# In a visit to the array's quarters, k^T v's even chunks go off the diagonal and its odd ones on it

## The chip, the cores and the metric

The kernel runs on one core of a Trainium2 chip. A core has five engines that run side by side: TensorE (PE in the profile; its weight loads are listed apart as PEld), VectorE (DVE), ScalarE (ACT), GpSimd (POOL) and SyncE (SP, which here mostly issues DMA transfers). TensorE multiplies a stationary operand, loaded beforehand, with a moving one and adds the products up in PSUM, a memory of eight banks. SBUF is the larger memory that all engines work from. The metric is the device time of one execution in microseconds (us), lower is better.

## The reference

Two blocks follow each other. The first is a linear attention without softmax, followed by an RMS norm; the second is a feed-forward block with a gate:

```python
kv  = np.einsum('bhsd,bhse->bhde', k, v)          # q, k, v: (8, 8, 576, 64)
out = np.einsum('bhsd,bhde->bhse', q, kv)
rms = np.sqrt(np.mean(out * out, axis=-1, keepdims=True) + 1e-06)
x   = (out / rms * g_norm)                        # then (B,H,S,D) -> (B*S, H*D) = (4608, 512)
h = x @ w_in                                      # (512, 2048)
sp = np.maximum(h, 0.0) + np.log1p(np.exp(-np.abs(h)))
y = (h * erf(sp)) @ w_out                         # (2048, 512)
```

All is fp32. For each batch element and head, `kv` is a 64 x 64 matrix, summed over 576 rows of k and v.

## The kernel before, in words

**Rows.** Tokens are worked in nine groups of 512 (`NG = B + 1`): for each of the eight batch elements its first 512 rows, and a ninth group made of the last 64 rows of all eight. The groups are numbered T, and `attention(T, p)` does the attention of a pair of heads p (four pairs) of group T. While the feed-forward block works on group T, the attention of group T + 1 is prepared in pieces set between its steps, one pair of heads per quarter of the group.

**Feed-forward.** Groups 0 and (in part) 1 run as plain fp32 products (lines 1021 and 655). From then on operands are split into two fp32r parts and a third form, and each product is twelve matmuls of 128 x 512 (line 599, `product`): eight into a bank called `n_ps`, four into one called `m_ps`. Six PSUM banks are used in turn. ScalarE and VectorE clear them (lines 1192, 574, 569), apply the gate and cut the results for the second product. The weights in their three forms are kept in DRAM and loaded again for each group, on SP's DMA queue (`load_parts`, line 844).

**The visit.** Everything that the change touches lies in `visit()` inside `attention`, which TensorE reaches once for each pair of heads of groups 1 to 7, 28 times in all. Its output `at` is a PSUM tile of two banks. All its matmuls contract over 64 partitions (one head of the pair) and give 64 output partitions, so each uses one quarter of the 128 x 128 array: the quarter is named by the head whose rows go in (`rows_of[i]`) and by the half of the output partitions. Two quarters are on the diagonal (rows of head i to output half i), two off it (head i to half 1 - i). TensorE is given, in this order:

1. four products `kv^T q^T` of 64 x 256 (line 411), "the quarters": first two off the diagonal into bank 0, then two on it into bank 1;
2. two products of 64 x 64 for the last 64 rows of the batch element, "the tail" (line 419), both on the diagonal, into bank 1;
3. eighteen products of 64 x 64 (lines 425 and 343, `kv_products`), which make k^T v for the *next* pair of heads: nine chunks c of 64 rows, each for both heads i. A chunk lies either on the diagonal (and goes to bank 1) or off it (bank 0). The 28th visit has no next pair and leaves these out.

All products on one side add up in PSUM to a partial sum. VectorE later adds the partial sums of the two sides (`kv_kept`: two copies at line 360 and an addition at line 361), whichever chunks each holds. `kv_products` is also called by `prepare` (line 370), once, ahead of the first visit, and by `first_group` (line 702) for the four pairs of group 0; these calls have no quarters and no tail ahead of them.

**What sets the order.** The order is that of the program (a manual schedule): each engine gets its instructions in the order in which Python issues them, and waits on semaphores of the others. After the visit come ScalarE's square (line 430), VectorE's halving of the square (lines 447 and 448), the copy of the tail (line 433), `kv_kept`, and, a step later, the mean over 64 features on TensorE (lines 463 and 464) and the norm. TensorE itself goes on after the visit with the next product of the feed-forward block, which uses the whole array.

Of the kernel before, what the change touches and what calls it, by code (L numbers as in the profile page):

```python
# [68 lines left out]
def kernel(  # L69
# [253 lines left out]
    def halves_of(t):  # L323
        return t.rearrange("p (a t) -> p a t", a=2)
# [10 lines left out]
            qT = ready[T, p] = qt_tile("qT")  # L335
            nc.vector.transpose(out=qT, in_=q_sb.pop((T, p)))

    def kv_products(T, p, at):


        ks, vs = (x.pop((T, p)) for x in (k_sb, v_sb))
        for c in range(CH):
            for i, rows in enumerate(rows_of):
                half = (i + c) % 2
                yield partial(
                    nc.tensor.matmul,
                    at[rows_of[half], 1 if half == i else 0, kv_cols],
                    lhsT=ks[rows, c],
                    rhs=vs[rows, c],
                    start=(c < 2),  # L350
                    stop=(c >= CH - 2),
                )
# [10 lines left out]
    def at_tile():  # L363
        return at_pool(1).tile([P, 2, G], FP32, name="at_ps", tag="at")

    def prepare(T, p):

        at = at_tile()
        for product_ in kv_products(T, p, at):
            product_()  # L370
        kept.append(partial(kv_kept, T, p, at))
# [7 lines left out]
    def attention(T, p, in_parts=False):  # L379
# [6 lines left out]
        then = divmod(T * NP + p + 1, NP)  # L386

        def two(t):
            return halves_of(t) if quad else t
# [14 lines left out]
        def visit():  # L404


            qT = ready.pop((T, p))
            at = st["at"] = at_tile()
            x = halves_of(qT[:, 0:G])
            for a, i in ((0, 0), (0, 1), (1, 0), (1, 1)):  # L410
                nc.tensor.matmul(  # L411
                    at[rows_of[i if a else 1 - i], a, 0 : 2 * P],
                    lhsT=bd[rows_of[i], a * D : (a + 1) * D],
                    rhs=x[rows_of[i], a],
                    start=True,
                    stop=True,
                )
            for s in rows_of:
                nc.tensor.matmul(
                    at[s, 1, 2 * P : 2 * P + R], lhsT=bd[s, D : 2 * D], rhs=qT[s, G:S], start=True, stop=True  # L420
                )
            st["o"] = at[:, :, 0 : 2 * P]
            if then[0] < B:
                for product_ in kv_products(*then, at):
                    product_()  # L425
            if apart:
                st["sq"] = x_new.tile([P, G], FP32, name="sq", tag="x")
            else:
                st["sq"] = qT[:, 0:G]
            nc.scalar.activation(two(st["sq"]), st["o"], AF.Square)  # L430
# [94 lines left out]
        if apart:  # L525
            pieces = ((loads,), (visit, halve, keep_tail), (then_,))
            return (*(partial(chain, *group) for group in pieces), mean, norm, *after)
        pieces = (first_, (visit, loads), (halve, keep_tail) if halves else (keep_tail,))
        return (*(partial(chain, *group) for group in pieces), mean, partial(chain, norm, then_), *after)

# [163 lines left out]
    def first_group(p):  # L694
# [4 lines left out]
        def kv():  # L699
            st["kv"] = at_tile() if p == 0 else ps_now[0].tile([P, 2, G], FP32, name="kv_ps", tag="at")  # L700
            for product_ in kv_products(0, p, st["kv"]):
                product_()
# [273 lines left out]
    for n in range(FIRST * FC + 1):  # L976
        T, f = divmod(n, FC)
# [165 lines left out]
    for m in range(first_batch, batches + 1):  # L1143
        T, b = divmod(m, NB)
# [141 lines left out]
```

## Time and profile before

| what | value |
|---|---|
| time, median of 3 runs | 902.89 us (902.69 to 903.44) |
| span of the profiled execution, first to last instruction | 901.3 us |
| mean granted TensorE clock | 0.999 |
| TensorE busy, share of the span | 893.6 us, 99% |
| VectorE busy | 766.7 us, 85% |
| ScalarE busy | 595.1 us, 66% |
| mean of one record of line 425 (k^T v in a visit) | 221 ns |
| distance between visits, groups 3 to 7 | 23.81 us |

The profiled execution is one run, and of its time the page gives the span; the timed runs also hold what lies around it. In the rows that follow, a group of instructions stands with its line, engine, operation, the names of output and inputs, the shape, how often, and after the bar the busy time in us, the mean of one in ns, and the idle time of its engine just before it. An fp32 matmul stands in the trace as two records, each with its own weight load: 18 products of a visit are 36 records, and 27 visits make 972. Matmuls overlap, so the duration of a record isn't its cost: what counts is the distance from one start to the next.

### The profile page before, as it was taken

The page shows a single profiled execution, that of the slowest core. Times are in us where ns is not written, and L with a number is a line of the kernel's source. Part 1 is how long each engine was busy: PE and PEld are TensorE (multiplying, and loading weights), DVE is VectorE, ACT ScalarE, POOL GpSimd, SP SyncE. Part 2 cuts the span into 40 slices and gives each one's busy share as a digit, 9 for nine tenths or more (in the row PEclk, how much of TensorE's full clock was granted, in tenths as well). Part 3 has the DMA queues.
Part 4 walks back from the last instruction along what each step waited for, and adds up shares of the span by engine and source line. Part 5 has one row for each costly group of instructions (what it writes and reads, how often), then busy time and mean ns, then how long its engine had stood idle before and what let it go on. Part 6 is the DMA issues. An engine that isn't in the chain of part 4 may idle for free.

```text
span 901.3 us, 13468 instructions
## 1 busy us (share of the span) xinstructions
PE 893.6 (99%) x4962; PEld 672.4 (75%) x4962; DVE 766.7 (85%) x1105; ACT 595.1 (66%) x789; POOL 4.7 (1%) x14
## 2 busy tenths in 40 slices
PE   8999999999999999999999999999999999999998
PEld 4444456666788888888888888888888888888887
DVE  5899978899799888888888888888888888886667
ACT  5976687777766666666766666666666666665552
POOL 2000000000000000000000000000000000000000
PEclk9999999999999999999999999999999999999999
DMA  9977418899699987988899979988897787778871
GB/s 285 295 224 226 108 73 319 305 341 355 233 384 355 347 301 258 382 308 297 273 361 336 320 248 335 365 300 292 286 341 273 270 304 309 286 282 323 317 263 51
DMA packets 136929, 259.89 MB, mean 288 GB/s; under 512 B 78816, under 2 KB 87264, under 8 KB 136864
## 3 DMA queue, kind: packets, MB, share of 16 engines
q1 hardware_dynamic: 136128, 258.09, 81.3%
q8 instruction: 39, 0.64, 0.3%
q10 hardware_dynamic: 544, 0.82, 0.3%
q14 instruction: 26, 0.21, 0.1%
q0 software_dynamic: 192, 0.13, 0.0%
HBM read 224.40 MB, written 34.60 MB: 287 GB/s over the span
## 4 chain that ended last, share of the span: by engine, by line
PE 96%; DMA 1%; DVE 1%; ACT 1%; issue 0%; SPq 0%; DVEq 0%
PE n_ps L599 50%; PE m_ps L599 25%; PE o_ps L655 9%; PE h_ps L1021 5%; PE at_ps L425 2%; PE at_ps L411 2%; PE n_ps L918 1%; PE at_ps L463 1%; PE at_ps L464 1%; DMA q_sb<-in_q_dram 1%; DMA w_raw<-in_moe_w_out_dram 1%; PE o_ps L918 0%; DVE w_e L276 0%; PE o_ps L722 0%; DVE w_in_sb L281 0%; PE ms_ps L729 0%
## 5 line engine op out<-in xcount | busy, mean ns | idle before, releaser
L599 PE MATMUL n_ps<-w_out_parts,g_forms 128*128 128x512 f32 (+1 forms) x936 | 230.7, 389 | 0.0
L599 PE MATMUL n_ps<-x_forms,w_in_parts 128*128 128x512 f32 x896 | 223.9, 392 | 0.0
L599 PEld LDWEIGHTS n_ps<-w_out_parts,g_forms 128*128 128x128 f32 x936 | 173.7, 188 | 35.3
L599 PEld LDWEIGHTS n_ps<-x_forms,w_in_parts 128*128 128x128 f32 x896 | 166.6, 188 | 35.3
L574 DVE TENSOR_TENSOR h<-m_ps,h 128x512 f32<-128x512 f32 x116 | 78.2, 687 | 60.3 <-PE m_ps L599 58.1
L599 PE MATMUL m_ps<-w_out_parts,g_forms 128*128 128x512 f32 x464 | 124.0, 389 | 0.0
L599 PE MATMUL m_ps<-x_forms,w_in_parts 128*128 128x512 f32 x448 | 119.7, 389 | 0.0
L1192 ACT ACTIVATE h<-n_ps 128x512 f32<-128x512 f32 x112 | 66.2, 594 | 75.1 <-PE n_ps L599 75.0
L1197 ACT ACTIVATE s<-h 128x512 f32<-128x512 f32 x112 | 68.3, 629 | 70.0 <-DVE h L574 70.0
L599 PEld LDWEIGHTS m_ps<-w_out_parts,g_forms 128*128 128x128 f32 x464 | 87.1, 188 | 18.5
L599 PEld LDWEIGHTS m_ps<-x_forms,w_in_parts 128*128 128x128 f32 x448 | 84.1, 188 | 17.5
L574 DVE TENSOR_TENSOR e<-m_ps,e 128x512 f32<-128x512 f32 x116 | 80.2, 692 | 15.2 <-PE m_ps L599 5.3
L655 PE MATMUL o_ps<-w_out_sb,h_sb 128*128 128x512 f32 x192 | 86.8, 595 | 0.0
L540 DVE SCALAR_TENSOR_TENSOR g_forms<-g_forms 128x1024 fp32r<-128x1024 f32 x58 | 71.1, 1225 | 2.0
L537 DVE TENSOR_TENSOR g_forms<-h,g_forms 128x1024 fp32r<-128x1024 f32 x58 | 70.6, 1217 | 1.2 <-ACT g_forms L534 1.1
L534 ACT ACTIVATE g_forms<-h 128x1024 fp32r<-128x1024 f32 x58 | 58.4, 1049 | 15.5 <-PE m_ps L599 11.1
L569 DVE SCALAR_TENSOR_TENSOR e<-n_ps,e 128x512 f32<-128x512 f32 (+1 forms) x89 | 60.4, 678 | 6.9 <-PE n_ps L599 6.9
L1246 DVE TENSOR_TENSOR h<-h,s 128x1024 f32<-128x1024 f32 x56 | 65.9, 1218 | 0.0
L655 PEld LDWEIGHTS o_ps<-w_out_sb,h_sb 128*128 128x128 f32 x192 | 35.5, 190 | 38.3 <-issue 36.9
L1021 PE MATMUL h_ps<-xT,w_in_sb 128*128 128x512 f32 x128 | 57.9, 596 | 1.1 <-DVE w_in_sb L281 1.1
L115 ACT ACT_TABLE_LOAD x43 | 55.2, 1283 | 0.8
L1220 ACT ACTIVATE s<-s 128x1024 f32<-128x1024 f32 x50 | 50.6, 1053 | 0.3
(148 smaller groups left out, 1018.7 us busy)
## 6 DMA issues: line engine op xcount, KB each, us to landing
w_out_parts<-w_out SPq DMA_DIRECT2D x116, 768.0 KB, 6.8
w_in_parts<-w_in SPq DMA_DIRECT2D x112, 768.0 KB, 6.7
w_in<-w_new SPq DMA_DIRECT2D x16, 768.0 KB, 4.9
k_sb<-in_k_dram SPq DMA_DIRECT2D x32, 288.0 KB, 5.9
v_sb<-in_v_dram SPq DMA_DIRECT2D x31, 288.0 KB, 5.8
w_raw<-in_moe_w_in_dram SPq DMA_DIRECT2D x16, 512.0 KB, 5.9
w_raw<-in_moe_w_out_dram SPq DMA_DIRECT2D x8, 1024.0 KB, 5.1
out_dram<-e SPq DMA_DIRECT2D x32, 256.0 KB, 3.8
```

The lines of the kernel that those rows point to most:

```text
L115: nc.scalar.preload_act_table_set("softplus")
L534: nc.scalar.activation(high, x, AF.Copy, scale=1.0 + 2.0**-13)
L537: nc.vector.tensor_tensor(out=low, in0=x, in1=high.bitcast(FP32), op=ALU.subtract)
L540: nc.vector.scalar_tensor_tensor(out=both, in0=low.bitcast(FP32), scalar=SHIFT, in1=high.bitcast(FP32), op0=ALU.mult, op1=ALU.add,)
L569: nc.vector.scalar_tensor_tensor(out=out_, in0=ps, scalar=scale, in1=out_, op0=ALU.mult, op1=ALU.add)
L574: nc.vector.tensor_tensor(out=out_, in0=ps, in1=out_, op=ALU.add)
L599: nc.tensor.matmul(ps[:, cols], lhsT=weights(form, k), rhs=moving(form, k)[:, cols], start=(form == forms[0] and k == 0), stop=(form == fo ...
L655: nc.tensor.matmul(o_ps[j], lhsT=g[:, j * P : j * P + P], rhs=one(w_out_sb, f), start=(f == 0), stop=last,)
L1021: nc.tensor.matmul(plain[i], lhsT=blocks_of(one(w_in_sb, i % FC))[:, c], rhs=xT[T][:, c, :], start=(c == 0), stop=(c == KC - 1),)
L1192: nc.scalar.activation(h[:, i], n_ps, AF.Copy, scale=SHIFT - 1.0)
L1197: nc.scalar.activation(s[:, i], h[:, i], AF.Softplus)
L1246: nc.vector.tensor_tensor(out=part(h, half), in0=part(h, half), in1=part(s, half), op=ALU.mult)
```

## The change

The call of `kv_products` in the visit gets `first=1`, which turns the sides around: chunks 0, 2, 4, 6 and 8 go off the diagonal, into bank 0, and chunks 1, 3, 5 and 7 on it, into bank 1. The tail stays on the diagonal. The other callers keep `first=0`. The number of instructions of every kind, their shapes, their operands in SBUF and their order in the program stay as they were.

```diff
-    def kv_products(T, p, at):
+    def kv_products(T, p, at, first=0):
 
         ks, vs = (x.pop((T, p)) for x in (k_sb, v_sb))
         for c in range(CH):
             for i, rows in enumerate(rows_of):
-                half = (i + c) % 2
+                half = (i + c + first) % 2
                 yield partial(
                     nc.tensor.matmul,
                     at[rows_of[half], 1 if half == i else 0, kv_cols],
                     lhsT=ks[rows, c],
                     rhs=vs[rows, c],
                     start=(c < 2),
                     stop=(c >= CH - 2),
                 )
...
             if then[0] < B:
-                for product_ in kv_products(*then, at):
+                for product_ in kv_products(*then, at, first=1):
                     product_()
```

## The prediction

> **What bounds the kernel now.** I read the page's busy times first, then the chain of work that ended last, then the groups of the visit's three lines, and last the timeline around single visits. From the page:
>
> ```profile
> span 901.3 us, 13468 instructions
> PE 893.6 (99%) x4962; PEld 672.4 (75%) x4962; DVE 766.7 (85%) x1105; ACT 595.1 (66%) x789; POOL 4.7 (1%) x14
> PE 96%; DMA 1%; DVE 1%; ACT 1%; issue 0%; SPq 0%; DVEq 0%
> ```
>
> TensorE is busy for 99% of the span and makes 96% of the chain, so time taken from TensorE comes off the end, as long as nothing else becomes late. The groups by shape (busy us, mean ns, idle before):
>
> ```profile
> L425 PE MATMUL at_ps<-v_sb,k_sb 64*64 64x64 f32 x972 | 23.0, 221 | 0.0
> L411 PE MATMUL at_ps<-qT,bd_kv 64*64 64x256 f32 x224 | 18.6, 402 | 0.0
> L419 PE MATMUL at_ps<-qT,bd_kv 64*64 64x64 f32 x112 | 7.9, 217 | 0.0
> ```
>
> Line 425 costs 23.0 us over 27 visits, 0.85 us each; this is where the change can take from. TensorE's timeline of one visit of the steady part (start us, length us, records):
>
> ```profile
> 287.76 0.66 PE L411 MATMUL at_ps<-qT,bd_kv 64*64 64x256 f32 x8
> 288.26 0.22 PE L419 MATMUL at_ps<-qT,bd_kv 64*64 64x64 f32 x2
> 288.27 0.27 PE L425 MATMUL at_ps<-v_sb,k_sb 64*64 64x64 f32 x2
> 288.32 0.23 PE L419 MATMUL at_ps<-qT,bd_kv 64*64 64x64 f32 x2
> 288.37 0.75 PE L425 MATMUL at_ps<-v_sb,k_sb 64*64 64x64 f32 x34
> 289.05 0.50 PE L599 MATMUL n_ps<-x_forms,w_in_parts 128*128 128x512 f32 x1
> ```
>
> Two records of line 425 start between the tail's first and second pass. The tail and chunk 0 share the diagonal quarters, so these two can only be chunk 1, off the diagonal: it overtook chunk 0. The record with chunk 0's semaphore wait, a weight load at 554 ns (counted, as all ns below, from the visit's first product at 287.764), says the same. So each quarter of the array works off its own products, and the visit lasts as long as the longer of two chains. Its end, in the same view with the window moved, so that the first number is the start of the earliest record still running:
>
> ```profile
> 288.73 0.40 PE L425 MATMUL at_ps<-v_sb,k_sb 64*64 64x64 f32 x9
> 288.78 0.34 PE L425 MATMUL at_ps<-v_sb,k_sb 64*64 64x64 f32 x6
> 288.90 0.23 PE L425 MATMUL at_ps<-v_sb,k_sb 64*64 64x64 f32 x2
> ```
>
> The last six records fill three places, two records each, where earlier places hold four: at the end only the diagonal works. And the visit without k^T v:
>
> ```profile
> 692.97 0.28 PE L419 MATMUL at_ps<-qT,bd_kv 64*64 64x64 f32 x4
> 693.18 0.50 PE L599 MATMUL n_ps<-x_forms,w_in_parts 128*128 128x512 f32 x1
> ```
>
> There the whole-array product comes 148 ns after the last small start (559 to 707 ns in the rows); with k^T v it is also 148 (1142 to 1290). So the end of the visit is the last small start plus a fixed emptying of the array.
>
> **The change part by part.** *The two chains now.* On the diagonal, starts (first of two heads) are 496 and 552 (tail, two passes), then 610, 669, 727, 785, 844, 902, 960, 1019, 1077, 1135 (five chunks, two passes each): twelve places, 58.3 ns apart once running. Off the diagonal: 509, 615, 674, 732, 790, 849, 907, 965 (four chunks): eight places, done three places early. The change removes one chunk, two places, from the diagonal and adds two places off it: ten and ten. Nothing else is added or removed; no DMA, no instruction of VectorE, ScalarE or SP changes or moves in its queue.
>
> *Diagonal after.* It loses its last two places and ends with 1019 (second head 1025): 1142 - 1025 = 117 ns earlier.
>
> *Off the diagonal after.* The unknown is when chunk 0 starts. Its quarters begin the second pass of the big products at 267 and 274; the diagonal's begin at 280 and 287, and the tail follows 216 ns later (496 - 280 = 503 - 287), its weights having been loaded beside them at 282 and 289. By the same step chunk 0 starts at 267 + 216 = 483, its second pass 56 later (as 496 to 552), and eight more places give 483 + 56 + 8 x 58.3 = 1005; second head 1012. The diagonal, at 1025, then sets the end: saving 117 ns, the upper bound. Lower bound: the weights come as late as chunk 1's do now (507 ns, right behind the tail's second load at 504). Then the places are 509, 615 and eight more: 615 + 8 x 58.3 = 1081, second head 1088, saving 54 ns.
>
> I take 117. What held chunk 1 back to 507 was how far TensorE reaches over unissued records. At 507 it passed 10 (the two tail matmuls, eight records of chunk 0); at 854 chunk 7's first load passed 11; before 496 it would have had to pass 14 and did not. In the new order chunk 0 stands directly behind the tail: at 282 it has at most 8 ahead (one big matmul, seven of the tail). That is inside what the rows show as passable. k and v are there: their loads land microseconds before, and chunk 1 of the same tiles is read at 509 now.
>
> The Trainium skill, "TensorE: Matmul & The Clock Gate", Part 3 (packing small matmuls), says that matmuls start and end strictly in program order, and that a weight load overlaps running matmuls only in other row groups. Both speak against this forecast: chunk 0 would wait for the tail's second pass at 559, start about 561 and end near 1090, worth some 52 ns a visit or 1.35 us in all, 901.5 us. The trace disagrees on both: chunk 1 starts at 509, ahead of the tail's 552; and the tail's loads at 282 run beside big products on the same rows (267, 280).
>
> *What waits for the visit.* ScalarE's square, VectorE's copies and the release of k's and v's buffers wait for the visit's last product and can come 117 ns earlier; nothing queues behind a new wait. For the rest, cover must last: VectorE is busy 398.5 of the 452.3 us from 240.2 to 692.5, ScalarE 295.5, and TensorE 452.3, with no idle gap. The weight loads land at least 2.6 us ahead of first use there, and they are triggered mostly by TensorE's own progress. If that cover were gone, at most the saving itself would be lost.
>
> *One visit gives nothing.* After the first visit (at 41.5 us) TensorE waits for VectorE; the chain there:
>
> ```profile
> 49.87 1.24 DVE w_in_sb L281
> 51.15 1.12 PE h_ps L1021 x2
> ```
>
> TensorE sat idle 0.39 us for it, and that VectorE chain comes from a DMA issued by SP at 42.34, not from the visit; the first 117 ns only lengthen the wait. From 51.15 on the chain is TensorE's to the last stretch.
>
> *Sum.* 26 visits x 0.117 = 3.04 us; 26 x 0.054 = 1.40 us at the lower bound; 27 x 0.117 = 3.16 at the upper. The profiled span of 901.3 would become 898.3. The median of the timed runs, 902.89, stands 1.6 us above that span, for what lies around it, which the change leaves alone: 902.89 - 3.04 = 899.85.
>
> **The rivals.** *A, the forecast:* 899.85 us.
>
> *B, late start off the diagonal:* chunk 0's first weight load carries the wait on a DMA's semaphore, and no row shows such a load taken ahead of older ones. If it isn't, it goes at 507, in order. Against it: at 139.27 a load of line 599 with a wait is issued 1 ns after the matmul before it starts. 902.89 - 1.40 = 901.49 us, 0.16% faster.
>
> *C, the change does not show in the time:* something other than the chains holds the next product, which has a semaphore wait of its own at 1289. For it: VectorE and ScalarE, which it waits for, are busy through the visit. Against it: it comes 148 ns after the last small start in every visit, with and without k^T v; a foreign wait would scatter. 902.9 us.
>
> *D, slower:* four quarters working at once run at a longer place than two, and the change makes ten such places of eight. At the start of the program the four places of group 0 (5.15 to 5.63) are 107 ns apart. At that distance ten places (nine distances, 963 ns) take the place of the present twelve (1135 - 496 = 639 ns): 324 ns more, 26 x 0.324 = 8.4 us, 911.3 us. It decides from about 79 ns a place, (639 + 69) / 9, where 69 ns a visit is 0.2%. Against it: in that same group the distance falls to 58 by 5.71 with four records a place; the same eighteen products ahead of the first visit (37.12) run at 58, four at once, and so do the eight shared places in this visit.
>
> **How the numbers follow.** About 0.2%, 1.8 us, is what a measurement of this kernel can tell from no change. A has 0.74, B 0.15, C 0.07, D 0.04. A is faster; B and C are within the bound; D is slower; a little of B lies between the two bounds of the start and beyond 0.2%: faster 0.75, same 0.21, slower 0.04. A's own range is 899.4 to 900.5 (27 visits and the runs' spread below, a chain start some 20 to 40 ns late above). To leave out no more than 2 in 10 I take in B: 899.4 to 901.7.
>
> **What would show it.** In the profile after, line 425 begins ahead of line 419 in the timeline, about 483 ns after the first quarter; the last places hold four records; the next product comes at 1173 ns instead of 1290; visits in the steady part are 23.69 us apart instead of 23.81. Line 425's busy time stays near 23 us or less, since it begins sooner but ends earlier. A start at 509 and a next product near 1236 would show B; places longer than 58 ns, D; a gap above 148 ns, C. The forecast is wrong if TensorE takes a waiting load only in order, or if VectorE's chain in groups 1 and 2, where it is busy 82.9 of 93.4 us, sets the pace instead.

## The result

The changed kernel is faster by 0.23%: 900.96 us (median of 12 runs, 900.4 to 901.16) against 902.93 us (12 runs), ratio 0.9977, 95% interval 0.9969 to 0.9986. Two later sessions gave 0.9975 (0.9966 to 0.9984) and 0.9973 (0.9962 to 0.9985). The saving is 2.0 to 2.5 us; 3.04 had been forecast. The result lies inside the range that was given (899.4 to 901.7), 1.1 us above the forecast of 899.85.

### The profile after

From the page; the span was 901.3 before:

```profile
span 899.1 us, 13468 instructions
PE 891.6 (99%) x4962; PEld 670.6 (75%) x4962; DVE 765.5 (85%) x1105; ACT 594.8 (66%) x789; POOL 4.7 (1%) x14
PE 97%; ACT 2%; DVE 1%; issue 0%; DVEq 0%; ACTq 0%
```

TensorE is 2.0 us less busy and still makes the chain. The groups by shape:

```profile
L425 PE MATMUL at_ps<-v_sb,k_sb 64*64 64x64 f32 x972 | 20.5, 218 | 0.0
L411 PE MATMUL at_ps<-qT,bd_kv 64*64 64x256 f32 x224 | 18.6, 402 | 0.0
L419 PE MATMUL at_ps<-qT,bd_kv 64*64 64x64 f32 x112 | 7.9, 217 | 0.0
```

Only line 425 moved: 23.0 to 20.5 us, its mean from 221 to 218 ns. The timeline of the same visit on TensorE (first product at 287.131):

```profile
287.13 0.66 PE L411 MATMUL at_ps<-qT,bd_kv 64*64 64x256 f32 x8
287.61 0.22 PE L425 MATMUL at_ps<-v_sb,k_sb 64*64 64x64 f32 x2
287.63 0.22 PE L419 MATMUL at_ps<-qT,bd_kv 64*64 64x64 f32 x2
287.67 0.23 PE L425 MATMUL at_ps<-v_sb,k_sb 64*64 64x64 f32 x2
287.68 0.23 PE L419 MATMUL at_ps<-qT,bd_kv 64*64 64x64 f32 x2
287.73 0.65 PE L425 MATMUL at_ps<-v_sb,k_sb 64*64 64x64 f32 x32
```

Chunk 0 now starts ahead of the tail, and a first and second pass of each alternate. Row by row, in ns from the visit's first product, the weights of chunk 0 are loaded at 268 and 275, its products start at 482 and 489, the tail's at 496 and 502, the last four of the visit at 1005, 1011, 1018 and 1025, and the next whole-array product at 1173. The forecast had 483, 1005, 1025 and 1173. All 27 visits show the same, within 1 or 2 ns.

So where is the rest of the 3.04 us? The busy times by stage, cut at the first visit, at the ninth (where the steady part begins) and at the last. The columns are the stretch and its length, then the busy time (and number of instructions) of PE, PEld, VectorE, ScalarE and GpSimd, and at the end the granted clock, the busy share of the DMA engines and the GB/s that they moved. Before:

```profile
41.48:240.15 198.67, 198.05 (x961) 114.30 (x961) 176.65 (x268) 147.59 (x210) 0.00 (x0) 1.00 0.69 235
240.15:692.48 452.33, 452.33 (x2814) 370.19 (x2813) 398.52 (x571) 295.52 (x381) 0.00 (x0) 1.00 0.91 319
692.48:901.30 208.82, 205.19 (x921) 170.01 (x920) 164.38 (x210) 122.27 (x154) 0.00 (x0) 1.00 0.72 270
```

After:

```profile
41.64:239.70 198.06, 197.32 (x961) 113.58 (x960) 176.48 (x268) 147.46 (x210) 0.00 (x0) 1.00 0.68 235
239.70:690.26 450.56, 450.56 (x2814) 368.50 (x2813) 397.61 (x571) 295.40 (x382) 0.00 (x0) 1.00 0.92 321
690.26:899.10 208.84, 205.19 (x921) 170.00 (x920) 164.29 (x210) 122.25 (x154) 0.00 (x0) 1.00 0.71 270
```

The steady part lost 1.77 us over 19 distances between visits, 93 ns each and not 117, and TensorE has no idle gap in it either way. From visit to visit the distances changed so: first to second +4 ns; the next three -133, -118 and -117; the three after these, in group 1's feed-forward, only -40 each; then -120; then nineteen at -93. Set row beside row, the matmuls that follow are longer. In the steady part, before and after, the first feed-forward product behind the visit, and the start of the one behind it:

```profile
289.05 2.11 PE L599 MATMUL n_ps<-x_forms,w_in_parts 128*128 128x512 f32 x8
291.91 0.84 PE L599 MATMUL n_ps<-x_forms,w_in_parts 128*128 128x512 f32 x3
```

```profile
288.30 2.12 PE L599 MATMUL n_ps<-x_forms,w_in_parts 128*128 128x512 f32 x8
291.18 0.84 PE L599 MATMUL n_ps<-x_forms,w_in_parts 128*128 128x512 f32 x3
```

The twelve matmuls take 2.852 us before and 2.875 after (by the rows' ns). Their distances settle at 226.7 ns. Before, the first is 338 and those that follow 236, 228, 232, 231, then 227; after, the first is 335, then 235, 233, 236, 224, 231, 236, 228, 233, 231, and only then 227. Added up over the ten behind the first, that is 20 to 21 ns above the settled pace before and 46 to 47 after, 23 ns net of the 2 to 3 saved on the first. In the three distances of -40 the same happens on a larger scale: the first split product behind the visit (a few plain ones of line 655 come ahead of it) runs at 225 and 228 ns in turn before, at 234 and 239 after; 77 of the 117 ns go there. Together 3 x 77 + 19 x 23 = 0.67 us are given back; this loss is called the give-back below, and the 20 to 21 or 46 to 47 ns above the settled pace the excess.

### The profile page after: what moved, and what is told of

It reads as the page before. It is cut to its first block, busy times and chain, and to the rows that moved or that the text cites. A ratio compares the mean times of both kernels' runs of the same rounds, so it can differ in the third digit from the quotient of the medians.

```text
span 899.1 us, 13468 instructions
## 1 busy us (share of the span) xinstructions
PE 891.6 (99%) x4962; PEld 670.6 (75%) x4962; DVE 765.5 (85%) x1105; ACT 594.8 (66%) x789; POOL 4.7 (1%) x14
## 4 chain that ended last, share of the span: by engine, by line
PE 97%; ACT 2%; DVE 1%; issue 0%; DVEq 0%; ACTq 0%
PE n_ps L599 50%; PE m_ps L599 25%; PE o_ps L655 9%; PE h_ps L1021 5%; PE at_ps L411 2%; PE at_ps L425 2%; PE n_ps L918 1%; PE at_ps L463 1%; PE at_ps L464 1%; PE warm_ps L802 1%; PE o_ps L918 0%; ACT w_m L260 0%; PE o_ps L722 0%; DVE w_in_sb L281 0%; DVE w_e L276 0%
```

## The experiments

The question left was what decides the give-back: how the visit ends (two quarters at work or four), how short it is, or when it ends. The kernels ran in three sessions, each on another chip and each with the kernel before beside them. Of the first four kernels there is one timed run each, so that their times say little and the argument rests on their traces; of the others there are 6 to 11.

**The tail left out, sides as before.**

```diff
-            for s in rows_of:
-                nc.tensor.matmul(
-                    at[s, 1, 2 * P : 2 * P + R], lhsT=bd[s, D : 2 * D], rhs=qT[s, G:S], start=True, stop=True
-                )
...
-                out=x_last[:, p, T * R : T * R + R], in_=st["at"][:, 1, 2 * P : 2 * P + R]
+                out=x_last[:, p, T * R : T * R + R], in_=st["at"][:, 1, 0:R]
```

The copy behind the visit then reads columns that the quarters wrote, in the tail's place.

> The kernel before with its sides as they were, but the tail's two products of the visit are left out (the last 64 rows of each batch element then come out of other numbers). Chain theory: the diagonal falls from twelve places to ten, 496 to 1018/1025 ns after the visit's first product, off the diagonal stays at eight; the next product at 1173 ns, as in the changed kernel, though no chunk has changed sides. Rival (the changed kernel is faster because four quarters, not two, are at work at the end): the visit loses less than 117 ns. On the give-back behind the visit (9 to 11 products some ns longer, 23 ns in the steady part): if it hangs on when the visit ends, the first distance is 335 ns and the excess of the next ones over 226.7 is 46 ns, as in the changed kernel; if it hangs on the diagonal working alone at the end, 337 to 338 and 20 to 21 ns, as in the kernel before.

```profile
287.73 0.66 PE L411 MATMUL at_ps<-qT,bd_kv 64*64 64x256 f32 x8
288.21 0.76 PE L421 MATMUL at_ps<-v_sb,k_sb 64*64 64x64 f32 x36
288.90 0.50 PE L595 MATMUL n_ps<-x_forms,w_in_parts 128*128 128x512 f32 x1
```

Measured: last start 1025, next product 1173 ns in every visit; 335 ns and 46 to 47 behind it; 23713 ns from visit to visit in the steady part, the changed kernel's figure to the nanosecond. The diagonal worked alone for the last places here, as in the kernel before, and still the give-back was the changed kernel's. So the saving is the length of the longer chain, whichever products are taken off it, and the give-back does not come from the quarters that are at work at the end. The time, 901.46 us against 903.2, holds 0.67 us lost in one wait, told of below.

**Odd chunks ahead of even ones.** In the changed kernel:

```diff
-        for c in range(CH):
+        order = (1, 0, 3, 2, 5, 4, 7, 6, 8) if first else range(CH)
+        for n, c in enumerate(order):
```

> The changed kernel, ten places on each side, with chunk 1 (on the diagonal) issued ahead of chunk 0 (off it), 3 ahead of 2 and so on. If what lets chunk 0 start at 483 is that it stands within TensorE's reach behind the tail, it now stands behind 16 records and starts at 509 without weights loaded ahead: last start near 1088, next product near 1236 ns, 63 ns a visit and 1.7 us in all lost against the changed kernel. If balance alone counts and the order does not, 1173 ns and the changed kernel's time.

```profile
287.24 0.66 PE L412 MATMUL at_ps<-qT,bd_kv 64*64 64x256 f32 x8
287.73 0.22 PE L420 MATMUL at_ps<-qT,bd_kv 64*64 64x64 f32 x2
287.75 0.27 PE L426 MATMUL at_ps<-v_sb,k_sb 64*64 64x64 f32 x2
...
288.48 0.50 PE L600 MATMUL n_ps<-x_forms,w_in_parts 128*128 128x512 f32 x1
```

The first two records of k^T v start behind the tail's and last 0.27 us, as in the kernel before; the next product came at 1236 to 1237 ns. With the same ten places on each side, the order alone costs 63 ns in the visit. Here the semaphore's wait stands with chunk 1 on the diagonal, and chunk 0, free of any wait, is late all the same: it is the distance in the queue that holds it back. The kernel without the tail says the same from the other side: there chunk 1 off the diagonal had 11 unissued records ahead of it, chunk 0's with the wait among them, its weights were loaded at 268 all the same, and its first product started at 483. That the wait does no harm is shown by the changed kernel, where the load at 268 carries it. The give-back was gone, though: 337 to 338 ns and 20 to 21 behind the visit, so the distance between visits is 23753 ns, only 40 above the changed kernel's. Time 901.67 us against 903.2.

**One more product per quarter.** Ahead of k^T v in the changed kernel's visit (for two more, the range is 2):

```diff
+                spare = slice(2 * P + R + D, 2 * P + R + 2 * D)
+                ks, vs = k_sb[then], v_sb[then]
+                for n in range(1):
+                    for side in (0, 1):
+                        for i, rows in enumerate(rows_of):
+                            half = i if side else 1 - i
+                            nc.tensor.matmul(
+                                at[rows_of[half], side, spare],
+                                lhsT=ks[rows, n], rhs=vs[rows, n], start=True, stop=True,
+                            )
```

> The changed kernel with one more product of 64 x 64 for each quarter in every visit, into PSUM columns that nothing reads: twelve places on each side. Chain theory: next product at 1290 ns, 117 more, time as before the change, some 3 us above the changed kernel. On the give-back: if it hangs on when the visit ends, 337 to 338 ns and an excess of 20 to 21 ns, as in the kernel before, whose visit ends at the same distance; if on four quarters being at work at the end, 335 and 46 ns.

Measured: last start 1142, next product 1290 ns, 337 to 338 ns and 20 to 21, 23806.6 ns from visit to visit: in all of these the kernel before, with 56 matmul records in the visit instead of 48, and twelve places on each side instead of twelve on the diagonal and eight off it. Four more products per visit off the diagonal cost nothing while they fit beside the diagonal. Time 904.26 us against 903.2, 0.86 us of it lost in the wait told of below.

**Two more per quarter.** The three distances so far suggested a raster, so that this run had a forecast that could fail:

> The changed kernel with two more products of 64 x 64 for each quarter in every visit, into columns that nothing reads: fourteen places on each side. Chain theory: next product at 1406 to 1407 ns. Theory of a raster for the give-back: in the kernels so far the distance of two steady visits differs from the 23806.6 ns of before by 53.3, 93.3 and 126.7 ns, all multiples of 6.67; a visit that ends a whole number of 6.67 ns earlier or later (0, 53.3, 126.7) is followed by 337 ns and an excess of 20 to 21, one that ends half a step off (116.7 is 17.5 steps) by 335 and 46 ns. Here the visit ends 116.7 ns later than before, half a step off: 335 and 46 ns again, 23946.7 ns from visit to visit. Rival (a shorter visit costs the products behind it, for want of instructions fetched in time): 337 and 20 ns, 23923 ns.

Measured: next product at 1406 to 1407 ns; 335 ns and 46 to 47; 23946.6 ns from visit to visit. A longer visit than that of the kernel before gives back just as the shorter one does, so it is not the shortness. Time 906.25 us against 902.94. The kernels side by side, in order of the visit's end:

| kernel | next product, ns | shift against before, in 6.67 ns | first distance, ns | excess, ns | visit to visit, ns |
|---|---|---|---|---|---|
| joined tail (next) | 1163.4 | -19.0 | 337 to 338 | 20 to 21 | 23680.0 |
| changed | 1173.4 | -17.5 | 335 | 46 to 47 | 23713.3 |
| tail left out | 1173.3 | -17.5 | 335 | 46 to 47 | 23713.3 |
| odd ahead of even | 1236.7 | -8.0 | 337 to 338 | 20 to 21 | 23753.3 |
| before | 1290.0 | 0 | 337 to 338 | 20 to 21 | 23806.6 |
| one more each | 1290.0 | 0 | 337 to 338 | 20 to 21 | 23806.6 |
| two more each | 1406.7 | +17.5 | 335 | 46 to 47 | 23946.6 |

Every distance between visits of the steady part differs from that of before by a whole number of 6.67 ns (-19, -14, -8, 0, +21), and a visit that ends half a step off is put back on the raster at 23.3 ns, 3.5 steps, by the products behind it.

The traces hold two more tests of this. The give-back of group 1 sorts the kernels in the same way: the split product there runs at 225 and 228 ns in the kernels that end a whole number of steps off (before, odd ahead of even, one more each, and the joined tail from its sixth visit on) and at 234 and 239 in the three that end half a step off. So the two give-backs go together in these kernels. But behind the 28th visit, which has no k^T v, two values are not enough. With the tail in place the next product comes at 706 to 707 ns, 87.5 steps ahead of 1290, and 335 to 336 ns and an excess of 46 to 47 follow, as the raster wants. With the tail left out or joined it comes at 593 or 699, and 335 ns are followed by 40 to 41, a third value that the raster as put does not have.

**The tail joined to the quarter.** The tail has the weights of the diagonal quarter products and the columns next to theirs, in SBUF and in PSUM:

```diff
-            x = halves_of(qT[:, 0:G])
...
-                    at[rows_of[i if a else 1 - i], a, 0 : 2 * P],
+                    at[rows_of[i if a else 1 - i], a, 0 : 2 * P + R * a],
                     lhsT=bd[rows_of[i], a * D : (a + 1) * D],
-                    rhs=x[rows_of[i], a],
+                    rhs=qT[rows_of[i], a * 2 * P : a * 2 * P + 2 * P + R * a],
...
-            for s in rows_of:
-                nc.tensor.matmul(
-                    at[s, 1, 2 * P : 2 * P + R], lhsT=bd[s, D : 2 * D], rhs=qT[s, G:S], start=True, stop=True
-                )
```

> The changed kernel with the tail's product joined to the quarter that has the same weights and the neighbouring columns: two products of 64 x 320 on the diagonal in place of 64 x 256 and 64 x 64. Chain theory: a pass of 64 columns inside a longer product takes 53 ns and not a place of 58, and two places go: the diagonal ends near 1015 instead of 1025, so next product near 1163 ns, 10 ns a visit and 0.3 us in all, give or take what the products behind the visit do (up to 26 ns a visit either way). If a product of 320 columns costs more than its columns, no gain or a loss of some 50 ns a visit.

Measured: next product at 1163 to 1164, and on the good side of the raster: 23680 ns from visit to visit, 33 less than the changed kernel. The time was 900.46 us (6 runs), ratio 0.997 (0.9957 to 0.9982). To tell it from the changed kernel, both ran again together:

> The changed kernel once more, beside the joined tail on the same chip: next product at 1173 ns, 23713 ns from visit to visit, 0.23% faster than before within some 0.1%.

> The kernel with the joined tail once more: next product at 1163 to 1164 ns, on the raster (126.7 ns is 19 steps), so 337 and 20 ns behind it and 23680 ns from visit to visit; 26 visits at 10 ns and 20 to 24 of them at a further 23 to 77 give 1.0 us less than the changed kernel, if its median is not moved by something else: 0.3 to 0.35% faster than before.

The changed kernel: 900.56 us, ratio 0.9975 (0.9966 to 0.9984). The joined tail: 900.61 us, 0.9974 (0.9964 to 0.9984). By visits it is a good 0.9 us ahead, but in both of its profiles TensorE waits once in the first quarter of group 2, which the changed kernel does not in any of its three profiles. TensorE's timeline there, of the joined tail in the second session (in brackets the idle time and what ended it):

```profile
245.58 1.52 PE L594 MATMUL n_ps<-w_out_parts,g_forms 128*128 128x512 f32 x6
247.70 0.73 PE L594 MATMUL n_ps<-w_out_parts,g_forms 128*128 128x512 f32 x2 [0.59 <-DMA w_out_parts<-w_out]
```

The fourth load of w_out's forms lands at 247.66, 9.9 us after it was issued; TensorE would have needed it about 246.9. In the kernel before it took 8.8 us and landed 0.58 us ahead of its use, in the changed one 8.7 us and 0.58. The kernels with the tail left out and with one more product each had the same wait in their one profile, 0.67 and 0.86 us, so it isn't the joined tail's alone, nor a matter of a shorter visit. (The 0.67, 0.86 and here 0.89 us are what the distance between the two visits grows by; the idle time in the trace is shorter by 0.2 to 0.3 us.)

**Loads of k, v and q later.** In the joined tail:

```diff
-            fetch_some(2)
+            if m > first_batch or place > 2:
+                fetch_some(2)
```

> The kernel with the joined tail, and in the first quarter of group 2 the loads of k, v and q are issued three steps later, behind the four loads of w_out's forms that TensorE needs first. In two of two profiles of the joined tail, and in one each of two other kernels, TensorE waits 0.7 to 0.9 us for the fourth of these loads. Theory (those loads share the DMA engines with k, v and q): the wait goes, the distance of the first two visits of the steady part is near 23.68 instead of 24.57 us, and the kernel comes near 899.7 us, 0.35% faster than before. Rival (the fourth load is late by itself): the wait stays and the time with it, near 900.6 us.

> The changed kernel beside it on the same chip: 0.23% faster than before, 900.5 to 901.0 us, 0.8 to 1.0 us slower than the one with the joined tail and later loads, if that one loses its wait.

Measured: the wait stayed (first distance of the steady part 24.77 us). With k and v out of the way SP issued two loads of w_in's forms and the next one of w_out at 239.25 to 240.23, earlier than before, and the fourth load took 10.2 us. So the theory that k, v and q make it late fails as it was put. It is no clean test of sharing, though: what was issued in the place of k and v (288 KB each) were loads of 768 KB. Time 900.29 us, ratio 0.9971 (0.9961 to 0.9982); the changed kernel beside it 900.58 us, 0.9973 (0.9962 to 0.9985). The two can't be told apart. Why the fourth load takes 8.7 to 8.8 us in some kernels and 9.8 to 10.2 in others was not settled.

## Why the prediction was right, and where it was off

- *Two chains, twelve places against eight.* Right, to the nanosecond: 1025 and 1173. The run without the tail and the one with one more product each show it from both sides.
- *Chunk 0 starts at 483, because it stands within reach of the queue.* Right: 482 to 483. The order swapped gives 1236, where the reasoning had put the late start (lower bound, rival B). The reach itself was only bounded: 11 records were passed (in the kernel before at 854 ns, without the tail at 268) and 14 were not.
- *The first visit gives nothing.* Right: the distance to the second is 4 ns longer, and TensorE's wait for VectorE's `w_in_sb` is 0.51 us instead of 0.39. In the changed kernel the path into that wait was not the one that the prediction named: the chain in its profile runs through ScalarE's work from 40.48 us on and through the first visit's square (line 430, at 45.65 us), not through the DMA issued at 42.34.
- *26 visits x 117 ns.* Here the sum failed: the term was taken as if the products behind the visit kept their length. They gave back 77 ns three times and 23 ns nineteen times, 0.67 of 3.04 us; 2.38 us is left between the first visit and the end (859.85 to 857.46 us), and 2.2 in the span, since the first visit came 0.16 us later in this execution (in the eleven profiles it lies anywhere between 40.57 and 42.11).
- *Cover.* VectorE, ScalarE and the weight loads kept up, and TensorE has no idle gap in the steady part of the changed kernel. But one figure behind this was misread: the weight loads do not all land at least 2.6 us ahead of their use. The fourth of w_out's forms landed at 247.79 us in the kernel before and its first product started at 248.37, 0.58 us later. In the changed kernel the load came as much earlier as TensorE did and 0.58 us was left again; in five profiles of other kernels the load took longer, and TensorE waited.
- *Rivals.* B, C and D are out. The strict program order of matmuls that the Trainium skill states ("TensorE: Matmul & The Clock Gate", Part 3) would by the prediction's estimate have ended the visit near 1090 and given a next product near 1238; 1173 was measured. Of rival D, the places of group 0 are 107 ns apart only from 5.31 us on; the first distance, from 5.15, is 161. Its price was not needed: with four quarters at work the places stayed 58 ns apart.

What could have been seen before: the last visit, without k^T v, was followed by 335 ns and an excess of 46 ns in the trace of before too, the others by 338 and 20. Two visits of different length behaved differently behind their end, and the forecast looked only at the 148 ns up to the next product.

## What to carry to other kernels

Small products that each use a quarter of the array run as separate chains, one for each quarter: count the places per quarter, put the odd remainder on the emptier ones, and issue first what goes to the quarter that is free soonest, since the engine looks past only some ten records (here 11 were passed, 14 were not). A saving read from one stretch of an engine that is never idle must be checked against the distance to the next repetition of the loop, because the products behind can run at another pace. And a version that is ahead by every visit is not yet faster: a single wait of 0.9 us elsewhere took all of the joined tail's gain.

## What the runs showed of the hardware

- From the ninth visit on, matmuls of 128 x 512 that follow a switch from quarters to the whole array take 5 or 10 distances to settle at 226.7 ns: a first one of 335 to 338 ns, then some of 224 to 236. Which of the two it is goes with when the switch comes, in half steps of 6.67 ns. The raster is a description of seven kernels' distances, one of them forecast; it does not cover the 28th visits of the kernels whose tail was left out or joined, and what makes it was not found.
- In group 1 one and the same product runs at 225 and 228 ns or at 234 and 239 ns, by the same half steps, with the same instructions on VectorE and ScalarE beside it, their lengths within 2 ns (sixth visit, before and after).
- A weight load that carries a semaphore's wait was taken ahead of older loads of other quarters (268 against 281 ns in the changed kernel), and matmuls on different quarters start out of program order in every visit with k^T v, before (509 ahead of 552) and after (482 ahead of 496).
- Two products of 64 columns joined to two of 256 saved 10 ns a visit; a place of its own costs 58 ns, the same columns inside a longer product some 53.
